# One DMA transpose in place of eight TensorE transposes, for one chunk of a linear-attention and mixer kernel

## The chip, the cores and the metric

The kernel runs on one core of one Trainium2 chip. The metric is device time in microseconds (us) for one launch, as the median of several executions. Lower is better.

## What is computed

The inputs `r`, `k` and `v` have 4 batches, 8 heads, 768 time steps and a head width of 48. First comes a linear attention with a decaying state, then a mixer over tokens and channels. Cut to what matters:

```python
for t in range(S):                      # per batch and head
    cur = (u * k[t]) outer v[t]
    y[t] = r[t] @ (state + cur)
    state = w * state + k[t] outer v[t]
x = y, heads side by side               # 4 x 768 x 384
h = relu(x^T @ w_tok1) @ w_tok2         # mixes the 768 steps
u = x + h^T
out = u + relu(u @ w_ch1) @ w_ch2       # mixes the 384 channels, 1536 hidden
```

## The kernel before

**Tiles.** The 768 steps of a batch are cut into 6 chunks of 128 steps, so there are 24 units (batch, chunk), counted from 0. "Batch 2" below is the third batch, and (2, 0) is its first chunk. A unit computes its chunk of `y` in the following way. `k` and `r` are scaled by powers of the decay (`kr`, half 0 for `k`, half 1 for `r`), both halves are turned so that the head width lies on the partitions (`rk`), and the turned halves are multiplied to scores (`at_ps`) for the 128 x 128 pairs of steps. VectorE masks the scores (`AT`), and TensorE multiplies them by `v` in bf16 (`vb`) and adds the part of the carried state `S` (`y_ps`). The sums of `k` outer `v` go into a bank of PSUM of their own (`kv_ps`), of which there is one; every third chunk of batch 2 closes a group, VectorE makes `S` from the bank, and the next group's first `kv_ps` sums are written into the same bank. A step's own term (`u`) goes another way: GpSimd makes `ku` and `rku`, VectorE sums `rku` per head to `adg`, GpSimd multiplies by `vb` to `yd`, and VectorE adds `yd` to `y_ps` and writes `x_b`.

**The two ways to turn.** The table `STYLES` says for each unit how `k` and `r` are turned. In `unit` (line 815) the style `'pe'` calls `turn_all` (line 903): eight 128 x 128 transposes by TensorE into a PSUM bank (`tr_ps`), and a copy of 128 x 1024 by VectorE or ScalarE into `rk` (`evac`, line 909). The style `'dma'` calls `turn_rk` (line 896): one DMA transpose from SyncE's queue, from `kr` in SBUF to `rk` in SBUF. The style also names who sums the own term; `'dve'` is the same in both.

```python
def turn_rk():
    L["rk"] = sb("rk", [128, 2, HP, T], bf16)
    sp.dma_start_transpose(L["rk"].rearrange("p j a s -> p (j a) s"),
                           L["kr"].rearrange("p j h d -> p (j h d)"))
```

In batches 2 and 3 units go in pairs (`GROUPS`): the scores of (2, 0) and (2, 1) are 16 matmuls in one step, then those of (2, 2) and (2, 3), then (2, 4) and (2, 5). Before the change the two units of the first pair are turned by TensorE, all ten behind them by DMA. In these two batches the products on `k` and `r`, and `ku`, `rku` and `yd`, are on GpSimd (`POOL_ONLY`).

**The mixer** (line 1013) of one batch runs among the attention of the next: `h_ps` stands in the profile for three sums (over `x_b` and `wtok`; over `zr` and `wch`, which is the output; and its addition by `ident`), `hx_ps` and `hT_ps` for the second token matmul, `z_ps` for the hidden channels, `zr` for their relu on ScalarE or VectorE, `osb` for an output tile that SyncE's queue stores. There are three `osb` buffers; a fourth output waits for the store of the buffer that it takes.

**The order.** All steps are recorded as tasks and then issued in the order of a table, `ORDER`; `InOrder` (line 287) keeps that order on each engine, so every instruction has line 287 in the profile. Further tables say which buffer each tile takes (`BUFS`; `m` is the seven banks of PSUM) and, where two engines could do a step, which one does (`ENGINES`). SyncE's queue issues all loads (`kt`, `rt`, `vt`; `win` for two chunks of `r` at once), all DMA transposes and all but one of the stores, one behind the other in this order. A load of `kt`, `rt` or `vt` is 192 KB in rows of 192 bytes; a DMA transpose of one unit is 256 KB.

Of the kernel before, what the change touches and what calls it, by code (L numbers as in the profile page):

```python
# [11 lines left out]
f32 = mybir.dt.float32  # L12
# [6 lines left out]
Ln = ACTF.Ln  # L19

ORDER = [
# [41 lines left out]
]  # L63
BUFS = {
    'AT0': [
# [41 lines left out]
],  # L107
    'osb': [
    0, 1, 2, 2, 1, 0, 2, 1, 2, 0, 1, 2, 0, 2, 0, 1, 0, 1, 2, 1, 0, 2, 1, 0, 2,
# [32 lines left out]
    0, 1, 2, 1, 0, 2,  # L142
],
    'yd': [
    0, 1, 2, 0, 1, 2, 0, 1, 2, 1, 2, 0, 1, 2, 0, 1, 2, 0,
],
    'ydb': [
    0, 1, 0, 1, 0, 1,
# [15 lines left out]
]  # L164
W_DEP = [(0, 2, 2), (0, 5, 0), (0, 5, 0), (0, 3, 2), (1, 2, 0), (1, 1, 2), (1, 3, 0)]
HOLD = {(0, 4, 1): (0, 2, 1),
# [28 lines left out]
 [(0, 1), (2, 3), (4, 5)]]  # L195
STYLES = [
  ('f32', 'pe'), ('f32', 'pe'), ('f32', 'pe'), ('f32', 'pe'), ('f32', 'pe'), ('f32', 'pe'), ('f32', 'pe'),
  ('f32', 'pe'), ('f32', 'pe'), ('f32', 'pe'), ('f32', 'pe'), ('f32', 'pe'), ('pe', 'dve'), ('pe', 'dve'),
  ('dma', 'dve'), ('dma', 'dve'), ('dma', 'dve'), ('dma', 'dve'), ('dma', 'dve'), ('dma', 'dve'),
  ('dma', 'dve'), ('dma', 'dve'), ('dma', 'dve'), ('dma', 'dve'),  # L200
]
# [1038 lines left out]
```

## Time and profile before

| what | value |
|---|---|
| median of 3 runs | 163.56 us (163.2 to 163.7) |
| the profiled execution, its own time | 162.75 us |
| its span, from the first to the last instruction | 161.0 us |
| TensorE busy | 153.0 us (95%), granted clock 0.997 |
| VectorE, GpSimd, ScalarE busy | 113.5, 89.3, 67.7 us |
| bytes moved by DMA | 26.35 MB, mean 164 GB/s |

A row of the timeline gives the start in us from the span's start, the duration, the engine, the operation, the tile written and the tiles read, and in brackets how long the engine had been idle before and what ended that. [...] PE is TensorE (PEld its weight loads), DVE VectorE, ACT ScalarE, POOL GpSimd. Buffer numbers are left out of the names.

### The profile page before, as it was taken

To read this page: it belongs to the slowest core of one execution; us is meant where nothing else is said; L and a number is where in the kernel's file an instruction comes from. 1 tells how busy PE (TensorE), PEld (TensorE's weight loads), DVE (VectorE), ACT (ScalarE), POOL (GpSimd) and SP (SyncE) were. 2 spreads that over 40 slices of the span, in tenths; PEclk is the share of its full clock that TensorE was granted. 3 is DMA by queue.
4 is the path that set the end of the run, shared out by engine and by line. 5 is a ranking of instruction groups with operands and counts; after the bars stand their busy time and mean duration, and the time that the engine had idled before them with its cause. 6 is when DMAs were issued, how large, how long until landed. Compare 5 with 4: busy or idle time off the path is not lost.

```text
span 161.0 us, 3815 instructions
## 1 busy us (share of the span) xinstructions
PE 153.0 (95%) x1475; PEld 102.1 (63%) x1475; DVE 113.5 (70%) x244; ACT 67.7 (42%) x150; POOL 89.3 (55%) x113
## 2 busy tenths in 40 slices
PE   6888789999999999999999999999999999999992
PEld 1354567776666777676776755766667666666661
DVE  6699695767574898789889876788988263852142
ACT  3977985567924243435144241047820202252000
POOL 7049892004788897999999998969422000000000
PEclk9999999999999999999999999999999999999998
DMA  4998899999999999999999997999620157200052
GB/s 124 202 213 165 149 206 211 210 209 196 224 210 211 173 232 178 252 236 171 186 193 224 196 184 150 240 201 197 137 77 4 49 122 219 98 4 0 0 195 98
DMA packets 90948, 26.35 MB, mean 164 GB/s; under 512 B 85682, under 2 KB 90036, under 8 KB 90932
## 3 DMA queue, kind: packets, MB, share of 16 engines
q1 hardware_dynamic: 88576, 22.88, 70.3%
q0 software_dynamic: 2160, 3.15, 11.7%
q8 instruction: 11, 0.18, 0.5%
q10 hardware_dynamic: 196, 0.11, 0.2%
q14 instruction: 5, 0.04, 0.1%
HBM read 20.46 MB, written 4.72 MB: 156 GB/s over the span
## 4 chain that ended last, share of the span: by engine, by line
PE 71%; DMA 10%; issue 9%; POOL 4%; ACT 2%; DVE 1%; SPq 1%; POOLq 0%
PE h_ps L287 34%; PE z_ps L287 23%; DMA vt<-in_v_dram 5%; DMA kt<-in_k_dram 5%; PE y_ps L287 4%; PE hT_ps L287 3%; PE at_ps L287 3%; PE kv_ps L287 2%; POOL wch L287 1%; POOL kr L287 1%; PE hx_ps L287 1%; PE tr_ps L287 1%; POOL pr L287 1%; PE trk L287 1%; ACT vb L287 1%
## 5 line engine op out<-in xcount | busy, mean ns | idle before, releaser
L287 PE MATMUL h_ps<-wch,zr 128*128 128x384 bf16 (+1 forms) x300 | 53.9, 320 | 0.0
L287 PE MATMUL z_ps<-uT,wch 128*128 128x384 bf16 x288 | 51.8, 326 | 0.0
L287 ACT ACTIVATE zr<-z_ps 128x384 bf16<-128x384 f32 x56 | 26.2, 492 | 41.8 <-PE z_ps L287 39.5
L287 PEld LDWEIGHTS <-wch 128*128 128x128 bf16 x288 | 31.4, 114 | 12.5
L287 PEld LDWEIGHTS <-zr 128*128 128x128 bf16 x300 | 27.4, 98 | 15.4 <-issue 0.2
L287 DVE TENSOR_TENSOR AT<-at_ps,mask 128x512 bf16<-128x512 f32 x48 | 30.6, 684 | 3.5 <-PE at_ps L287 2.9
L287 DVE TENSOR_SCALAR zr<-z_ps 128x384 bf16<-128x384 f32 x40 | 21.3, 553 | 12.5 <-PE z_ps L287 12.5
L287 POOL TENSOR_TENSOR kr<-kt,wnat 128x384 bf16<-128x384 f32 x20 | 19.9, 1005 | 2.8 <-DMA kt<-in_k_dram 2.7
L287 POOL TENSOR_TENSOR yd<-vb,adg 128x384 f32<-128x384 bf16 x17 | 13.9, 829 | 8.6 <-DVE x_b L287 4.2
L287 PEld LDWEIGHTS <-kr 128*128 128x128 bf16 x192 | 12.1, 97 | 6.8 <-DVE kr L287 1.8
L287 DVE TENSOR_TENSOR osb<-u_sb,h_ps 128x384 f32<-128x384 bf16 (+1 forms) x16 | 8.2, 526 | 9.7 <-PE h_ps L287 9.5
L287 ACT CAST vb<-vt 128x384 bf16<-128x384 f32 x22 | 11.0, 512 | 5.9 <-DMA vt<-in_v_dram 5.8
L287 POOL TENSOR_TENSOR rku<-ku,rt 128x384 f32<-128x384 f32 x12 | 12.0, 1000 | 0.2
L287 POOL TENSOR_TENSOR ku<-kt,u_bc 128x384 f32<-128x384 f32 x12 | 12.0, 1001 | 0.0
L287 POOL TENSOR_TENSOR kr<-rt,wp 128x384 bf16<-128x384 f32 x12 | 11.9, 1001 | 0.0
L287 DVE TENSOR_TENSOR x_b<-y_ps,yd 128x384 bf16<-128x384 f32 x18 | 9.5, 553 | 3.1 <-PE y_ps L287 1.4
L287 DVE TENSOR_TENSOR u_sb<-x_b,hT_ps 128x384 bf16<-128x384 bf16 x15 | 7.7, 551 | 4.5 <-PE hT_ps L287 4.4
L287 POOL DMA_DIRECT2D wch<-in_moe_w_ch_dram x5 | 3.4, 674 | 13.1 <-DMA kt<-in_k_dram 13.1
L287 PEld LDWEIGHTS <-wtok 128*128 128x128 bf16 x78 | 7.4, 98 | 4.5
L287 PE MATMUL h_ps<-x_b,wtok 128*128 128x384 bf16 x48 | 8.8, 326 | 0.0
L287 PE MATMUL y_ps<-vb,AT 128*128 128x48 bf16 x192 | 8.7, 183 | 0.0
L287 PEld LDWEIGHTS <-AT 128*128 128x128 bf16 x192 | 7.1, 96 | 0.3 <-DVE AT L287 0.2
(96 smaller groups left out, 180.4 us busy)
## 6 DMA issues: line engine op xcount, KB each, us to landing
kt<-in_k_dram SPq DMA_DIRECT2D x24, 192.0 KB, 4.2
vt<-in_v_dram SPq DMA_DIRECT2D x24, 192.0 KB, 4.0
out_dram<-osb SPq DMA_DIRECT2D x23, 192.0 KB, 2.2
win<-in_r_dram SPq DMA_DIRECT2D x6, 384.0 KB, 5.5
rt<-in_r_dram SPq DMA_DIRECT2D x12, 192.0 KB, 4.4
wch<-in_moe_w_ch_dram POOLq DMA_DIRECT2D x4, 384.0 KB, 6.1
wtok<-in_moe_w_tok_dram POOLq DMA_DIRECT2D x2, 384.0 KB, 6.8
wch<-in_moe_w_ch_dram POOLq DMA_DIRECT2D x1, 768.0 KB, 9.1
```

The costliest lines, as they stand in the source:

```text
L287: return lambda *args, **kw: tc.keep_in_program_order(f(*args, **kw))
```

## The change

`STYLES` gives unit 12, which is (2, 0), the style `('dma', 'dve')` in place of `('pe', 'dve')`. The eight transposes and the copy of that unit go, and one DMA transpose comes; there is one task less, so the numbers behind it in `ORDER` fall by one. `ORDER` also moves some steps of the same stretch, and `BUFS` (banks `m` and `yd`) and `ENGINES` follow. Unit (2, 1) is still turned by TensorE.

```diff
 ORDER = [
...
-    306, 411, 414, 407, 412, 394, 307, 416, 532, 429, 536, 89, 330, 415, 92, 422, 533, 395, 417, 419, 431, 313, 88,
+    306, 411, 414, 407, 412, 394, 307, 416, 532, 429, 536, 330, 415, 89, 395, 417, 419, 533, 92, 422, 431, 313, 396,
...
 STYLES = [
-  ('f32', 'pe'), ('f32', 'pe'), ('f32', 'pe'), ('f32', 'pe'), ('f32', 'pe'), ('pe', 'dve'), ('pe', 'dve'),
+  ('f32', 'pe'), ('f32', 'pe'), ('f32', 'pe'), ('f32', 'pe'), ('f32', 'pe'), ('dma', 'dve'), ('pe', 'dve'),
...
```

On SyncE's queue the place is behind the loads of `kt` for (2, 2) and (2, 3), about 60 us into the program. `kr_72` is the buffer with the products of (2, 0), `rk` the turned tile, and `out_dram<-osb` are stores of batch 0.

```order
@@ -27,8 +27,10 @@
 L287 DMA out_dram<-osb 128x384
 L287 DMA kt<-in_k_dram 128x8x48 x2
+L287 DMA_TRANSPOSE rk<-kr_72 128x8x128
 L287 DMA vt<-in_v_dram 128x8x48
+L287 DMA out_dram<-osb 128x384
 L287 DMA rt<-in_r_dram 128x8x48
+L287 DMA out_dram<-osb 128x384
 L287 DMA kt<-in_k_dram 128x8x48
-L287 DMA out_dram<-osb 128x384 x2
 L287 DMA rt<-in_r_dram 128x8x48 x2
 L287 DMA vt<-in_v_dram 128x8x48
```

The new transpose stands ahead of one load of `vt`, and so of all loads, transposes and stores behind that; the two stores, which stood together behind a `kt`, stand apart and earlier, the first ahead of an `rt` and the second ahead of the `kt`.

On VectorE the place is the stretch in which the mixer of batch 1 begins and the first scores of batch 2 are masked. `AT_` with a number is one masked tile of the scores, `u_sb` the mixer's sum, `zr` a relu.

```order
 L287 COPY rk<-tr_ps 128x1024
 L287 CAST uT<-hx_ps 128x3x128
-L287 TENSOR_TENSOR AT_1445<-at_ps,mask 128x512
-L287 TENSOR_TENSOR AT_1455<-at_ps,mask 128x512
 L287 TENSOR_TENSOR u_sb<-x_b_99,hT_ps 128x384
-L287 TENSOR_TENSOR AT_1474<-at_ps,mask 128x512
-L287 TENSOR_SCALAR zr<-z_ps 128x384 x3
+L287 TENSOR_SCALAR zr<-z_ps 128x384
+L287 TENSOR_TENSOR AT_1452<-at_ps,mask 128x512
+L287 TENSOR_TENSOR AT_1461<-at_ps,mask 128x512
+L287 TENSOR_TENSOR AT_1467<-at_ps,mask 128x512
+L287 TENSOR_SCALAR zr<-z_ps 128x384 x2
```

The masks of the first scores stand behind a `u_sb` and the first `zr` and no longer ahead of them, as on TensorE the 16 matmuls of these scores now stand behind four `hT_ps` and two groups of `z_ps`. The copy that is left is that of (2, 1); the one of (2, 0), a few rows further up, is gone. On ScalarE one `zr` moves ahead of a cast of `vb`. GpSimd's order is the same.

More of the change, by code (lines that the diff above doesn't have):

```diff
@@ L144 @@
     'yd': [
-    0, 1, 2, 0, 1, 2, 0, 1, 2, 1, 2, 0, 1, 2, 0, 1, 2, 0,
+    0, 1, 2, 0, 2, 1, 0, 1, 2, 1, 2, 0, 1, 2, 0, 1, 2, 0,
 ],
```

76 rows, old and new, of tables (BUFS, ENGINES, ORDER) are left out of this document.

## Prediction

> **What bounds the kernel now.** I read the page first, for the busiest engine and for the chain that ended last.
>
> ```profile
> span 161.0 us, 3815 instructions
> PE 153.0 (95%) x1475; PEld 102.1 (63%) x1475; DVE 113.5 (70%) x244; ACT 67.7 (42%) x150; POOL 89.3 (55%) x113
> ...
> PE 71%; DMA 10%; issue 9%; POOL 4%; ACT 2%; DVE 1%; SPq 1%; POOLq 0%
> ```
>
> TensorE is busy for 95% of the span and holds 71% of the chain. A share of the whole span does not say what bounds the stretch that the change touches, so the second view is the busy time in windows of 4 us around it. The columns are us, busy us (and count) of PE, PEld, DVE, ACT and POOL, granted clock, DMA share and GB/s.
>
> ```profile
> 64.00:68.00 4.00, 4.00 (x39) 2.86 (x38) 2.83 (x6) 1.75 (x5) 4.00 (x5) 1.00 0.99 242
> 68.00:72.00 4.00, 4.00 (x39) 2.63 (x37) 3.77 (x7) 2.03 (x5) 3.92 (x5) 1.00 1.15 243
> 72.00:76.00 4.00, 4.00 (x32) 2.74 (x31) 3.71 (x8) 1.75 (x5) 4.00 (x5) 1.00 0.93 166
> 76.00:80.00 4.00, 4.00 (x52) 2.84 (x50) 3.02 (x7) 1.27 (x4) 4.00 (x5) 1.00 0.95 180
> ```
>
> Three resources are full at once: TensorE 4.00 of 4 us, GpSimd 3.92 to 4.00, and the DMA engines at a share of 0.93 to 1.15. The end follows TensorE, since after 40 us its matmuls stand in the waits only once:
>
> ```profile
> PE trk L287 <- DVE kr L287: 0.2, 1, 0.2
> ```
>
> So a TensorE instruction that goes is worth its whole time, as long as nothing else comes late. And a DMA or a GpSimd step that slips is free only up to the slack that its reader has. The third view, the timeline of single engines, gives these slacks.
>
> **What goes.** The eight transposes of unit (2, 0) on TensorE, and their copy on VectorE:
>
> ```profile
> 63.21 0.61 PE L287 MATMUL tr_ps<-ident,kr 128*128 128x128 bf16 x8
> 63.66 2.11 PE L287 MATMUL h_ps<-x_b,wtok 128*128 128x384 bf16 x12
> 64.37 0.68 DVE L287 COPY rk<-tr_ps 128x1024 bf16<-128x1024 bf16 x1
> ```
>
> Matmuls overlap at their ends, so the price is start to start: 63.66 - 63.21 = 0.45 us of TensorE. The 12 matmuls behind it read `x_b`, which VectorE finishes by 64.4 us (the copy follows it) in the order that they want it, so starting 0.45 us sooner is possible. The 0.68 us of VectorE lie off the path there. Gain: 0.45 us at most; there is no other TensorE work removed.
>
> **What comes.** One DMA transpose on SyncE's queue, behind the two `kt` at 58.09:
>
> ```profile
> 58.09 1.32 SPq L287 DMA_DIRECT2D kt<-in_k_dram  x2
> 59.46 1.09 SPq L287 DMA_DIRECT2D vt<-in_v_dram  x1
> 60.60 1.72 SPq L287 DMA_DIRECT2D rt<-in_r_dram  x1
> 62.42 0.94 SPq L287 DMA_DIRECT2D kt<-in_k_dram  x1
> 63.41 1.19 SPq L287 DMA_DIRECT2D out_dram<-osb  x2
> 64.64 1.22 SPq L287 DMA_DIRECT2D rt<-in_r_dram  x2
> ...
> 71.36 4.01 SPq L287 DMA_TRANSPOSE rk<-kr  x2
> ...
> 80.22 2.67 SPq L287 DMA_TRANSPOSE rk<-kr  x2
> ```
>
> Its source and its readers:
>
> ```profile
> 57.33 1.00 POOL L287 TENSOR_TENSOR kr<-rt,wp 128x384 bf16<-128x384 f32 x1
> 68.44 0.62 PE L287 MATMUL at_ps<-rk 64*128 64x128 bf16 x16
> ...
> L287 SPq DMA_TRANSPOSE rk<-kr x10: 1232/1284/2666, 71.4 to 112.9; - x10
> DMA to landing us min/median/max: 3.1/3.4/4.7
> ```
>
> GpSimd has the second half of `kr` ready at 58.33, and the issue comes at 59.46. An `rk` lands 3.1 to 4.7 us after its issue, here by about 64, and the scores that read it start at 68.44 before, and behind more work after. So the transpose itself waits for nothing and nobody waits for it. What it costs is the queue. SyncE issues one DMA behind the other with hardly a gap (59.46 + 1.09 = 60.55, next at 60.60), and the engines behind are full, so everything behind 59.46 slips by the time that one transpose takes in the queue. No row isolates that, so I bound it:
>
> ```profile
> q1 hardware_dynamic: 88576, 22.88, 70.3%
> ```
>
> From below, its 256 KB (0.262 MB) at the best window's 243 GB/s are 1.08 us. The queue's mean gives 70.3% of 161.0 us over 88576 packets, 1.28 ns each; if a transpose is as many packets as a load (8 x 128 = 1024), that is 1.3 us. The shortest and the median issue are 1.23 and 1.28 us (the row of `rk<-kr` above, in ns). Of those in the full stretch, the pair at 80.22 took 2.67 us, 1.33 each, and the pair at 71.36 took 4.01 us, 2.0 each, the longest alone 2.67. I take 1.4 us, near most of these rows, and keep 1.08 to 2.0 for the range.
>
> [...]
>
> **Who feels the slip.** First ScalarE: it casts the `vt` issued at 59.46 and does the relu `h1r` behind it.
>
> ```profile
> vt<-in_v_dram SPq DMA_DIRECT2D x1, 192.0 KB, 4.9
> ...
> 64.08 0.93 ACT L287 CAST vb<-vt 128x384 bf16<-128x384 f32 x2
> 65.81 0.49 ACT L287 ACTIVATE h1r<-h_ps 128x384 bf16<-128x384 f32 x1 [0.80 <-PE h_ps L287]
> 67.20 0.49 PE L287 MATMUL hx_ps<-wtok,h1r 128*128 128x384 bf16 x2
> 68.11 0.49 ACT L287 COPY osb<-h_ps 128x384 f32<-128x384 f32 x1
> ```
>
> The `vt` landed at 59.46 + 4.9 = 64.4 and would land at 65.8; cast (0.5) and relu (0.5) are done at 66.8. TensorE wants the relu for the second of the two `hx_ps` matmuls, at 67.20 + 0.16 - 0.45 = 66.9. That is hidden, with nothing to spare; a longer transpose stalls TensorE here. The `osb` at 68.11 needs the second of the stores of 63.41; that store moves up past a `kt` (0.94) and down past the transpose (1.4), some 0.5 us later, so that `osb` may slip to 68.5 and the `uT` cast behind it by as much. The first `z_ps` behind that cast now stands ahead of the scores, at 68.44 - 0.45 and four `hT_ps` of 0.16, so about 68.65; its third matmul at about 69.0 needs the cast, so up to 0.3 us may stall here. These stalls take from the lead of 0.45 and are not added to the next one, which is the larger.
>
> Second GpSimd, through the first of the two `rt` at 64.64, the `r` of (2, 2). The change leaves that load behind the same DMAs as before, and the transpose.
>
> ```profile
> DMA to landing us min/median/max: 3.1/4.4/5.8
> rt<-in_r_dram SPq DMA_DIRECT2D x1, 192.0 KB, 3.8
> ...
> 67.69 1.00 POOL L287 TENSOR_TENSOR ku<-kt,u_bc 128x384 f32<-128x384 f32 x1
> 68.65 1.96 POOL L287 TENSOR_TENSOR kr<-rt,wp 128x384 bf16<-128x384 f32 x2
> ...
> 77.22 1.00 POOL L287 TENSOR_TENSOR rku<-ku,rt 128x384 f32<-128x384 f32 x1
> ...
> 78.25 0.55 DVE L287 TENSOR_REDUCE adg<-rku 128x8 f32<-128x384 f32 x1
> 78.72 0.55 DVE L287 TENSOR_TENSOR S<-kv_ps,wGm 128x384 bf16<-128x384 f32 x1
> ...
> 78.59 0.62 PE L287 MATMUL at_ps<-rk 64*128 64x128 bf16 x16
> ...
> 79.80 0.33 PE L287 MATMUL kv_ps<-vb,kr 128*128 128x96 bf16 x4
> ```
>
> GpSimd uses that `rt` at 68.65 without having waited. Its own landing is not shown: at the earliest 64.64 + 3.1 = 67.74, at the latest 68.65; the next `rt` landed 3.8 us after its issue at 65.22. I take 3.5 us, 68.14, which is 0.5 us of slack (bounds 0 and 0.9). With 1.4 us of slip GpSimd starts that product 1.4 - 0.5 = 0.9 us late. It has no idle time until past 80 (the windows above), so the `rku` of 77.22 ends at 78.22 + 0.9 = 79.1. VectorE's `adg` at 78.25 reads exactly that `rku` (it started 0.03 us behind it), and queued behind `adg` is `S`, which empties the one bank of `kv_ps`: `S` then ends at 79.27 + 0.9 = 80.17. TensorE's `kv_ps` of the next group, at 79.80 before, had 79.80 - 79.27 = 0.53 us of slack. It starts 0.9 - 0.53 = **0.37 us later than before**, though the transposes are gone: the lead of 0.45 us is used up and 0.37 us on top.
>
> Third the scores of (2, 2) and (2, 3) at 78.59, which need the second transpose of the pair at 71.36:
>
> ```profile
> 74.13 1.24 SPq L287 DMA_TRANSPOSE rk<-kr  x1
> ...
> rk<-kr SPq DMA_TRANSPOSE x1, 3.1
> ```
>
> It landed at 74.13 + 3.1 = 77.2 and would land at 78.6, against 78.59 - 0.45 = 78.14. That alone would leave TensorE where it was before; it comes ahead of the `kv_ps`, so the later one counts, not the sum.
>
> Behind 80 us TensorE has the same work as before and, running 0.37 us later, gives every reader that much more slack; the queue gets its time back where SyncE waits for the mixer's `u_sb`. So the sum is 162.75 + 0.37 = 163.1 us for a profiled execution. That execution was 0.8 us below the median of the runs shown, 163.56; on the median I forecast 163.56 + 0.37 = **163.9 us**.
>
> **The rivals.**
>
> *The queue takes it in: faster, 163.1 us.* If the transpose costs no more than 0.5 + 0.53 = 1.03 us of queue, GpSimd's lateness is inside the slacks, the scores' transpose lands at 78.2 and the gain of 0.45 us stays: 163.56 - 0.45. For it: the DMA share falls to 0.93 to 0.99 in three windows, so the queue may have holes that a transpose fills. Against it: the shortest issue of all ten is already 1.23 us, and the byte bound 1.08. [...] Chance 0.23.
>
> *The transpose costs what the pair at 71.36 cost: slower, 164.5 us.* With 2.0 us of slip (or 1.5 us and an `rt` that had landed just in time, with no slack), GpSimd is 1.5 us late and the `kv_ps` 1.5 - 0.53 = 0.97 us: 163.56 + 0.97. It decides from a lateness of GpSimd of 0.53 + 0.49 = 1.02 us on, which is only 0.1 us more than I take. For it: the first transpose of a run of two, ahead of which plain loads stand, was the long one, and the new one stands behind plain loads too; the window of 72 to 76 us has the fewest bytes, 166 GB/s. Against it: the median of the ten issues is 1.28 us. Chance 0.34.
>
> [...]
>
> That the change does not do what it says I leave out: the order shows the transposes gone and the DMA in place.
>
> **How the numbers follow.** The forecast of 163.9 us has a chance of 0.43, the faster rival 0.23, the slower one 0.34. The three runs before spread over 0.5 us, so a measurement can tell about 0.3% (0.49 us) from no change. The forecast, +0.37 us, lies within. The faster rival, -0.45 us, lies at the edge: half of it, 0.12, counts as faster, the rest, 0.11, as the same. So faster 0.12, same 0.43 + 0.11 = 0.54, slower 0.34. The range reaches from the whole gain, 163.1, to a lateness of 1.6 us, 163.56 + 1.6 - 0.53 = 164.6; the likeliest case's own range, with 1.1 to 1.5 us of slip, is 163.6 to 164.1.
>
> **What would show it.** Right: the eight `tr_ps` and one copy gone and `h_ps<-x_b` 0.45 us sooner; the two `rt` issued 1.2 to 1.6 us later; GpSimd idle for about 0.9 us ahead of a `kr<-rt`, with DMA as the releaser; VectorE waiting for GpSimd ahead of an `adg`, and the `kv_ps` behind the scores of (2, 2) no earlier than before. Wrong: GpSimd without that gap, or the scores of (2, 2) starting near 78.1, which is the faster rival; a gap of 1.5 us, which is the slower one; or a TensorE stall ahead of 70 us that alone exceeds 0.45 us, which would mean that ScalarE and not GpSimd carries the slip.

## The result and the profile after

The changed kernel is slower: 165.04 us median (164.5 to 165.6) against 163.63 for the kernel before beside it (163.2 to 163.75), a ratio of 1.0105 with a 95% interval of 1.0064 to 1.0145. The forecast was 163.9 with a range up to 164.6. The profiled execution took 164.5 us with a span of 162.8, against 162.75 and 161.0, so it shows 1.8 us of loss. The interval lies clear of 1; the loss is about 1% of the time.

First TensorE's waits after 40 us. The kernel before had only the `trk` row; three kinds have come.

```profile
PE at_ps L287 <- DMA rk<-kr: 0.8, 2, 0.5
PE hx_ps L287 <- ACT h1r L287: 0.6, 1, 0.6
PE trk L287 <- DVE kr L287: 0.2, 1, 0.2
PE kv_ps L287 <- DVE S L287: 0.2, 1, 0.2
```

Next SyncE's queue (SPq) in the timeline (start, duration of the issue). The row of 59.59 is the new transpose.

```profile
58.10 1.40 SPq L287 DMA_DIRECT2D kt<-in_k_dram  x2
59.59 3.31 SPq L287 DMA_TRANSPOSE rk<-kr  x1
62.96 0.57 SPq L287 DMA_DIRECT2D vt<-in_v_dram  x1
63.59 0.57 SPq L287 DMA_DIRECT2D out_dram<-osb  x1
64.20 0.43 SPq L287 DMA_DIRECT2D rt<-in_r_dram  x1
64.67 0.71 SPq L287 DMA_DIRECT2D out_dram<-osb  x1
65.43 0.43 SPq L287 DMA_DIRECT2D kt<-in_k_dram  x1
65.91 2.58 SPq L287 DMA_DIRECT2D rt<-in_r_dram  x2
...
73.79 3.75 SPq L287 DMA_TRANSPOSE rk<-kr  x2
...
82.49 2.70 SPq L287 DMA_TRANSPOSE rk<-kr  x2
```

Its issue took 3.31 us where the prediction took 1.4. The `vt` behind it starts 3.5 us later than before (62.96 against 59.46); the `rt` of (2, 2), five places further, only 1.3 us later (65.91 against 64.64); the pair of transposes for (2, 2) and (2, 3) is 2.4 us later again (73.79 against 71.36). So the slip is not one number for the whole queue. The landing was long as well; the DMA view of that stretch has

```profile
q8 instruction: 1, 0.02, 0.8%
...
rk<-kr SPq DMA_TRANSPOSE x1, 5.2
```

that is 5.2 us from issue to landing, with an instruction fetch (queue q8) in the same stretch. The windows of one us show that the DMA engines moved little just then; the last two columns are the DMA share and GB/s.

```profile
61.00:62.00 1.00, 1.00 (x21) 0.74 (x18) 0.91 (x3) 0.48 (x2) 0.94 (x2) 1.00 1.67 222
62.00:63.00 1.00, 1.00 (x20) 0.74 (x17) 0.97 (x2) 0.00 (x0) 0.45 (x1) 1.00 2.03 65
63.00:64.00 1.00, 1.00 (x11) 0.68 (x10) 1.00 (x3) 0.62 (x2) 0.69 (x1) 1.00 0.47 106
64.00:65.00 1.00, 1.00 (x8) 0.61 (x7) 0.38 (x1) 0.51 (x1) 1.00 (x2) 1.00 0.60 114
```

Who then came late, in the timelines of ScalarE, GpSimd and VectorE:

```profile
66.17 0.51 ACT L287 CAST vb<-vt 128x384 bf16<-128x384 f32 x1 [1.64 <-DMA vt<-in_v_dram]
66.70 0.49 ACT L287 ACTIVATE h1r<-h_ps 128x384 bf16<-128x384 f32 x1
...
70.28 1.97 POOL L287 TENSOR_TENSOR kr<-rt,wp 128x384 bf16<-128x384 f32 x2 [1.19 <-DMA rt<-in_r_dram]
...
79.90 0.55 DVE L287 TENSOR_REDUCE adg<-rku 128x8 f32<-128x384 f32 x1 [1.07 <-POOL rku L287]
80.37 0.55 DVE L287 TENSOR_TENSOR S<-kv_ps,wGm 128x384 bf16<-128x384 f32 x1
```

ScalarE waits for the `vt`, and the relu `h1r` stands behind that cast. GpSimd starts `kr<-rt` at 70.28 instead of 68.65, and VectorE's `adg` waits for GpSimd. On TensorE:

```profile
67.41 0.49 PE L287 MATMUL hx_ps<-wtok,h1r 128*128 128x384 bf16 x2
...
79.52 0.62 PE L287 MATMUL at_ps<-rk 64*128 64x128 bf16 x16 [0.28 <-DMA rk<-kr]
...
81.06 0.33 PE L287 MATMUL kv_ps<-vb,kr 128*128 128x96 bf16 x4 [0.16 <-DVE S L287]
...
88.88 0.62 PE L287 MATMUL at_ps<-rk 64*128 64x128 bf16 x16 [0.53 <-DMA rk<-kr]
```

To compare kernels that run some tenths apart from the start, I take the start of a TensorE group, less the start of the last `kv_ps` ahead of the change (63.04 before, 62.97 after), and subtract the same for the kernel before. For the scores of (2, 2) after: (79.52 - 62.97) - (78.59 - 63.04) = +1.00 us. Negative is ahead of the kernel before. The other columns are the runs below.

| TensorE group, its start before | after | no transpose | extra one | old order | five later | two later | loads behind | new queue |
|---|---|---|---|---|---|---|---|---|
| `h_ps` over `x_b`, 63.66 | -0.45 | -0.44 | 0.00 | -0.45 | -0.45 | -0.45 | -0.45 | -0.45 |
| first `hx_ps` that needs `h1r`, 67.20 | +0.28 | -0.44 | 0.00 | -0.25 | -0.44 | -0.44 | -0.44 | +0.09 |
| `kv_ps`, 72.09 | +0.67 | -0.13 | +1.25 | +1.24 | -0.14 | -0.09 | -0.03 | +1.53 |
| scores of (2, 2), 78.59 | +1.00 | -0.10 | +1.25 | +1.23 | +0.46 | +0.58 | -0.04 | +1.53 |
| next group's `kv_ps`, 79.80 | +1.33 | -0.10 | +1.25 | +1.24 | +0.47 | +0.98 | -0.03 | +1.53 |
| scores of (2, 4), 87.02 | +1.93 | +0.01 | +1.42 | +1.24 | +1.12 | +1.19 | +0.25 | +1.52 |
| scores of (3, 0), 100.75 | +1.87 | -0.04 | +1.37 | +1.23 | +1.06 | +1.13 | +0.20 | +1.52 |

The lead of 0.45 us is there at 63 us. It is lost at `h1r` (0.73), and more is lost up to 72 us (0.39), at the scores of (2, 2) (0.33), at `kv_ps` (0.33) and at the scores of (2, 4) (0.60). From there nothing changes.

### The profile page after: what moved, and what is told of

Read it like the earlier page. It is cut to its first block, busy times and chain, and to the rows that moved or that the text cites. A ratio compares the mean times of both kernels' runs of the same rounds, so it can differ in the third digit from the quotient of the medians.

```text
span 162.8 us, 3798 instructions
## 1 busy us (share of the span) xinstructions
PE 153.7 (94%) x1467; PEld 101.8 (63%) x1467; DVE 112.8 (69%) x243; ACT 67.9 (42%) x150; POOL 89.4 (55%) x113
## 4 chain that ended last, share of the span: by engine, by line
PE 59%; DMA 16%; issue 9%; POOL 8%; ACT 3%; SPq 2%; DVE 1%; POOLq 0%
PE h_ps L287 31%; PE z_ps L287 17%; DMA kt<-in_k_dram 8%; DMA vt<-in_v_dram 5%; POOL kr L287 4%; PE y_ps L287 3%; DMA rk<-kr 3%; PE hT_ps L287 3%; PE at_ps L287 2%; POOL yd L287 2%; SPq L287 2%; POOL wch L287 1%; PE kv_ps L287 1%; PE hx_ps L287 1%; POOL pr L287 1%
## 5 line engine op out<-in xcount | busy, mean ns | idle before, releaser
L287 DVE TENSOR_REDUCE adg<-rku 128x8 f32<-128x384 f32 x12 | 6.4, 545 | 1.5 <-POOL rku L287 1.5
```

What stands on the lines that cost most here:

```text
L287: return lambda *args, **kw: tc.keep_in_program_order(f(*args, **kw))
```

## The experiments

Theory Q: the DMA transpose delays what stands behind it in SyncE's queue, and the loss comes through the readers of those DMAs. Rival O: the new order of scores, stores and loads costs the time. A further question was why the issue was so long: theory F, because an instruction fetch met it; rival L, because plain loads were queued ahead of it. Ratios are to the kernel before on the same chip, with 95% intervals.

**No transpose.** The changed kernel with that one step left out: the scores of (2, 0) read a constant tile instead of `rk`.

```diff
 def turn_rk():
+    if n == 12:
+        plan.buf("rk")
+        L["rk"] = warm.rearrange("p (o a t) -> p o a t", o=1, a=HP)
+        return
     L["rk"] = sb("rk", [128, 2, HP, T], bf16)
```

> The changed kernel without its DMA transpose: the scores of (2, 0) read the constant zero tile `warm` instead of `rk`, so the scores of that chunk are left out; the moved order stays, and so do all loads and stores. Theory Q (the transpose delays all that stands behind it in SyncE's queue): without it the 0.45 us of TensorE remain as a gain, 163.63 - 0.45 = 163.2 us, `vt` issued near 59.5 as before, no wait of TensorE for `h1r`, `kv_ps` at 79.8 - 0.45 = 79.4 us. Rival O (the order in which scores, stores and loads now stand costs the time, the transpose itself does not): stays near 165.0 us, and `kv_ps` near 81.1.

Measured: 0.9996 (0.9962 to 1.003). The loss is gone, so the transpose carries it and rival O falls as the main cause. But the gain that Q left over does not show either: in the table 0.44 us are there at 67 us and 0.13 at 72 us. TensorE and VectorE in that stretch:

```profile
70.12 1.94 PE L287 MATMUL z_ps<-uT,wch 128*128 128x384 bf16 x9
71.90 0.33 PE L287 MATMUL kv_ps<-vb,kr 128*128 128x96 bf16 x4
```

```profile
70.03 1.89 DVE L287 TENSOR_TENSOR AT<-at_ps,mask 128x512 bf16<-128x512 f32 x3 [0.29 <-PE at_ps L287]
```

Nine `z_ps` matmuls take 71.90 - 70.12 = 1.78 us from start to start; before, twelve took 72.09 - 70.14 = 1.95, 0.1625 each, so nine should take 1.46. The 0.32 us between are lost at a `z_ps` that takes a bank of PSUM out of which VectorE must first mask the scores (`AT`): it waits for a semaphore of VectorE and starts at 71.38, right behind the end of the second mask at 71.32. The scores now come later, and three masks stand in a row up to 71.92 us. That is the price of the new order, 0.3 us, with no transpose in the queue.

**An extra transpose.** All of the kernel before, and a transpose of the same `kr` that nobody reads, ahead of the `vt` load (88 in the order).

```diff
+ extra.append((lambda: sp.dma_start_transpose(spare, L["kr"]...), [t_kp, t_rp]))
+ plan.order.insert(plan.order.index(88), 910)
```

> The kernel before, with all its TensorE transposes, its order and its scores, plus one DMA transpose of the same `kr` into a tile that nobody reads, at the place in SyncE's queue where the change puts its own (behind the two `kt` of 58 us, ahead of `vt`). Theory Q: the queue slips as in the changed kernel, TensorE has no 0.45 us to give, so 163.63 + 1.4 (after less before) + 0.45 = about 165.5 us, 164.8 to 166; an issue of about 3.3 us if theory F holds as well (the issue is long since an instruction fetch falls into it: the fetch comes at 60.4 us here too), about 1.4 us if it does not. Rival O: 163.6 us, no change.

Measured: 1.0071 (1.0037 to 1.0105), about 1.2 us: all else is the kernel before, so the one added DMA costs that. The issue took 3.20 us and the landing 5.4, as in the changed kernel.

```profile
59.63 3.20 SPq L287 DMA_TRANSPOSE wnpair<-kr  x1
```

The path is another one, though: in the table 1.25 us are lost between 67 and 72 us, nothing more at `kv_ps`, and 0.17 at the scores of (2, 4). The next run but one shows why.

**An extra load.** As above, with a plain load of 192 KB in place of the transpose.

```diff
+ extra.append((lambda: sp.dma_start(spare, k[b, :, ts(c, T), :]...), [t_kp, t_rp]))
```

> As the run with the extra transpose, but with a plain load of 192 KB of k in its place, which nobody reads. Theory F (a fetch and a transpose together stop the DMA engines, a fetch and a load do not): no second with under 150 GB/s between 60 and 65 us, an issue of 0.6 to 1.0 us, and a time of 163.6 to 164.1 us, since 0.8 us of slip is within the slacks of 0.5 us at `rt` and 0.5 us at `S`. If it is the bytes in the queue and not the transpose: 3/4 of its loss, about 165 us.

Measured: 1.0036 (1.0004 to 1.0067), 0.6 us, half of what the transpose costs. The issue took 1.88 us, more than expected, and the expectation that no window of 1 us (the "second" there) falls under 150 GB/s failed:

```profile
59.77 1.88 SPq L287 DMA_DIRECT2D spare<-in_k_dram  x1
```

```profile
62.00:63.00 1.00, 1.00 (x20) 0.83 (x18) 0.97 (x2) 0.00 (x0) 0.72 (x2) 1.00 0.59 112
```

So the DMA engines sag here with plain loads as well, in one window and not in three. The kernel before has 142 GB/s in this window, and the control run at the end, which has no new transpose, 33 GB/s. F holds in weaker form: the dip is longer with a transpose, not absent without.

**The transpose in the old order.** The DMA transpose at its place in the queue, with scores, stores and loads as in the kernel before.

```diff
  SyncE:  kt, kt,
+         transpose (2, 0),
          vt, rt, kt, out, out, rt, rt, ...
  TensorE:
-         tr_ps (2, 0)
          ... scores (2, 0), (2, 1), hT_ps, z_ps ...
```

> The transpose by DMA at the same place in SyncE's queue, but all else in the order of the kernel before: the scores of (2, 0) and (2, 1) ahead of the four `hT_ps` at about 68 us, the stores where they stood, the loads behind the transpose in the old order. Theory Q: 164.6 to 165.5 us, as the changed kernel or a little worse since the scores come 2 us sooner behind a landing at 64.8. Rival O: 163.2 us, the gain without the loss.

Measured: 1.0089 (1.0055 to 1.0122), within errors the changed kernel's 1.0105. So the transpose loses as much without the new order, by another path. VectorE's timeline, then TensorE's:

```profile
67.53 0.56 DVE L288 COPY osb<-h_ps 128x384 f32<-128x384 f32 x1 [2.28 <-DMA out_dram<-osb]
...
68.46 0.68 DVE L288 COPY rk<-tr_ps 128x1024 bf16<-128x1024 bf16 x1
```

```profile
68.14 0.38 PE L288 MATMUL at_ps<-rk 64*128 64x128 bf16 x7 [0.42 <-DVE osb L288]
69.20 0.40 PE L288 MATMUL at_ps<-rk 64*128 64x128 bf16 x8 [0.68 <-DVE rk L288]
```

VectorE waits 2.28 us for a store that slipped behind the transpose, since `osb` takes that store's buffer. Behind it waits the copy of (2, 1), and TensorE waits 0.42 + 0.68 = 1.10 us for both. The new order avoids this path (the scores come later, one store sooner) and pays elsewhere.

**Five places later.** The changed kernel with the transpose behind the `rt` of (2, 2) (93 in the order), which stands five places behind the `vt`; six DMAs in all now go ahead of it.

```diff
+ plan.order.remove(537)
+ plan.order.insert(plan.order.index(93) + 1, 537)
```

> The changed kernel with the transpose moved five places back in SyncE's queue: behind `vt`, both stores, the first two `rt` and a `kt`, at about 65.6 us; its readers, the scores at 69.6 to 70.4, leave it 4 us to land. Theory Q: no stall at `h1r` (0.7 us less), GpSimd's `kr<-rt` back near 68.6, but the loads and the pair of transposes behind slip; the scores of (2, 2) want that pair at 78.4 and it lands there without slack, so 0.4 to 0.9 us are lost there: with the 0.45 us of gain and the 0.3 us that the order costs, 163.6 + 0.2 to 0.7 us, some 1 us faster than the changed kernel. Theory F (a transpose that an instruction fetch meets takes 2 us more in the queue): the transpose at 65.6 takes 1.3 us and not 3.3. If it takes 3 us here too, plain loads ahead of it make it long, not the fetch.

Measured: 1.005 (1.002 to 1.008). As Q says, there is no stall at `h1r`, and GpSimd's `kr<-rt` starts at 68.41, with no wait. What stays is at the two pairs of transposes that stand behind the new one:

```profile
PE at_ps L287 <- DMA rk<-kr: 1.1, 2, 0.6
```

0.60 us at the scores of (2, 2) and 0.65 at those of (2, 4). The issue here took

```profile
64.80 2.08 SPq L287 DMA_TRANSPOSE rk<-kr  x1
```

and no fetch fell between 64.5 and 69 us. That lies between F's 1.3 and L's 3, so by this issue neither alone gives the length.

**Fetches shifted.** To move the fetches away, each warming matmul of 512 columns was cut into four.

```diff
-  pe.matmul(bank[0][:, 512 - cols:512], warm[:, 0:128], warm[:, 0:cols], ...)
+  for q in range(4):
+      pe.matmul(bank[0][:, ts(q, 128)], warm[:, 0:128], warm[:, 0:128], ...)
```

> The changed kernel with each of its twelve warming matmuls of 512 columns, all ahead of 16 us, cut into four of 128: the same columns, 36 more pairs of TensorE instructions, so that each instruction fetch comes 36 pairs sooner, about 3 us: 57.7, 70.1 and 82.9 us in place of 60.8, 73.8 and 86.3. Theory F: the transpose issued at 59.6 meets no fetch, takes 1.3 us in the queue and lands after 3.1 to 3.5 us; the loss shrinks from 1.9 us to 0.4 to 0.9 us, 164.0 to 164.5 on the scale where the kernel before has 163.6. Rival L (the plain loads queued ahead of it make it long): it takes 2.5 to 3.3 us as in the changed kernel, and the time stays at 165.0.

Measured: 1.0179 (1.0127 to 1.023). The control has the same lines in the kernel before:

```diff
-  pe.matmul(bank[0][:, 512 - cols:512], warm[:, 0:128], warm[:, 0:cols], ...)
+  for q in range(4):
+      pe.matmul(bank[0][:, ts(q, 128)], warm[:, 0:128], warm[:, 0:128], ...)
```

> The control of the run before: the same cut of the warming matmuls in the kernel before. Its transposes had slack, so neither theory sees more than 0.3 us of change: 163.3 to 163.9 on the scale where the kernel before has 163.6.

Measured: 1.0111 (1.0072 to 1.0151), with 2.1 us of wait for one `trk` before 50 us. The cut itself costs about 1.8 us, all of it ahead of the change, so as an experiment on time this pair failed, and so did the third of the kind, the transpose five places later with the cut:

```diff
+ plan.order.insert(plan.order.index(93) + 1, 537)
...
+  for q in range(4):
```

> The transpose five places later and the fetches 3 us sooner, both. Theory F: no transposes of the stretch from 65 to 79 us meet a fetch (57.7, 70.1, 82.9 us), the pair for (2, 2) and (2, 3) lands before its readers, and what stays is the 0.45 us of gain less the 0.3 us that the order costs: 163.3 to 163.6 us, no slower than the kernel before. Rival L: the long issue stays, and 0.4 us or more are lost at the scores of (2, 2), 164 us or more.

Measured: 1.0135 (1.0088 to 1.0181). Two things can still be read. With no fetch between its issue and its landing, the transpose of the first of these took 2.02 us and landed after 3.9.

```profile
60.65 2.02 SPq L287 DMA_TRANSPOSE rk<-kr  x1
```

Yet its `kv_ps` waited 1.2 us for `S`. The `rt` of (2, 2) was issued 0.66 us sooner than in the changed kernel ((65.73 - 63.45) - (65.91 - 62.97)), but now a fetch, at 68.82, fell into its landing, which took 5.6 us, and GpSimd waited for it:

```profile
71.36 1.96 POOL L287 TENSOR_TENSOR kr<-rt,wp 128x384 bf16<-128x384 f32 x2 [1.79 <-DMA rt<-in_r_dram]
```

A shorter issue alone does not save the time. Second, in the count of the table the last of the three stays 0.14 us ahead of the kernel before at the scores of (2, 2) and 0.15 at those of (3, 0), and the control stays at 0.00. That is the gain less the price of the order, as its expectation had it. It does not single out the fetch: TensorE had been held up at the start, so the queue stood 1.2 us further ahead of it than with the transpose five places later alone ((64.54 - 64.60) - (63.94 - 62.77) for that `rt`).

**Two places later.** Behind `vt` and a store (312 in the order), with the `rt` of (2, 2) still behind it.

```diff
+ plan.order.remove(537)
+ plan.order.insert(plan.order.index(312) + 1, 537)
```

> The changed kernel with the transpose two places back, behind `vt` and a store, at about 61.8 us; the `rt` of (2, 2) stays behind it. The instruction fetch at about 60.4 us is over by then. Theory F: 2.0 us in the queue and a landing 3.8 to 4.0 us after the issue, where the changed kernel had 3.3 and 5.2; if plain loads ahead alone decide, 2.6 to 3.3 us. Theory Q on the path: no wait of TensorE for `h1r`, but `kr<-rt` on GpSimd still 1.2 to 1.6 us late and `kv_ps` with it, 0.6 to 1.0 us behind where it stood before; in all 164.3 to 164.9 us on the scale where the kernel before has 163.6, between the run with five places (164.4) and the changed kernel (165.3).

Measured: 1.0082 (1.0051 to 1.0113), 1.3 us. The rows of the queue:

```profile
58.96 2.13 SPq L287 DMA_DIRECT2D vt<-in_v_dram  x1
61.14 0.79 SPq L287 DMA_DIRECT2D out_dram<-osb  x1
62.03 1.37 SPq L287 DMA_TRANSPOSE rk<-kr  x1
...
65.23 2.05 SPq L287 DMA_DIRECT2D rt<-in_r_dram  x2
```

The transpose now takes 1.37 us and lands after 3.2; the fetch, and the long issue, fell on the `vt` (2.13 us, against 0.57 in the changed kernel). No wait for `h1r`, but

```profile
69.38 1.95 POOL L287 TENSOR_TENSOR kr<-rt,wp 128x384 bf16<-128x384 f32 x2 [1.22 <-DMA rt<-in_r_dram]
```

GpSimd still waits for that `rt`, and `kv_ps` is 0.98 us behind. This separates the two paths: what stands directly behind the transpose loses through `h1r`, the `rt` further behind through GpSimd and `S`.

**Loads behind the pairs.** Five places later, and two `kt` with slack moved behind the pairs of transposes.

```diff
  SyncE:
-         vt, kt, transposes (2, 2), (2, 3), kt, uT, ..., transposes (2, 4), (2, 5)
+         vt, transposes (2, 2), (2, 3), kt, uT, ..., transposes (2, 4), (2, 5), kt
```

> The transpose five places back, and two `kt` with 4.5 and 15 us of slack moved behind the two pairs of transposes that came late there (0.6 and 0.65 us of TensorE at the scores of (2, 2) and of (2, 5)). Theory Q (the slip reaches TensorE through these pairs, as they stand behind it in the queue): both stalls shrink to under 0.2 us each, and what is left is the gain of 0.45 less the order's 0.3 to 0.4: 163.5 to 163.9 us on the scale where the kernel before has 163.6. If the pairs were late for another reason (the DMA engines full, a fetch), the stalls stay and the time is 164.4 as without this move.

Measured: 1.0031 (0.9997 to 1.0064): level with the kernel before within the errors, and 0.7% better than the changed one. Its interval overlaps that of the run five places later (1.002 to 1.008), so the time alone does not show a gain over that. The waits after 40 us:

```profile
PE trk L288 <- DVE kr L288: 0.2, 1, 0.2
PE at_ps L288 <- DMA rk<-kr: 0.2, 1, 0.2
```

The stall at (2, 2) is gone, that at (2, 4) fell from 0.65 to 0.28 us. So the slip did reach TensorE through these pairs. Its last matmul ends at 157.70 us (157.81 before), which counted as in the table is (157.70 - 62.26) - (157.81 - 63.04) = 0.67 us behind, so 0.47 us more are lost after 100 us; what causes that was not followed.

**The old order with a queue made for it.** Here the old order of the scores keeps the masks apart, and the queue is laid out so that what slips has slack; two `kt` go behind the pairs, as in the run before.

```diff
  SyncE:
-         kt, kt, transpose (2, 0), vt, rt, kt, out, out, rt, rt, ...
+         kt, kt, vt, out, out, rt of (2, 2), transpose (2, 0), rt, kt, rt, ...
```

> The transpose by DMA with the scores where they stood in the kernel before, and a queue laid out for it: `vt`, both stores and the `rt` of (2, 2) first, then the transpose at about 63.8 us, then the loads with slack, and the two `kt` behind the pairs. By theory Q no reader of the queue is late: the transpose lands at 67.7 us, where the scores want it at 68.0, and the whole 0.45 us stay as a gain, 163.2 us on the scale where the kernel before has 163.6, so the version that beats both. If the DMA engines and not the queue's order are what is full, something else comes late, and it is 163.6 us or more.

Measured: 1.0064 (1.0037 to 1.0092); Q's expectation failed, and the outcome is the one written down there for engines that are full whatever the order. The control has the kernel before, its TensorE transposes among it, and the same queue without the transpose:

```diff
  SyncE:
-         kt, kt, vt, rt, kt, out, out, rt of (2, 2), rt, ...
+         kt, kt, vt, out, out, rt of (2, 2), rt, kt, rt, ...
```

> The control of the run before: the kernel before, with its TensorE transposes, and that same queue without the transpose. TensorE waited for nothing there, so the new queue alone brings nothing: 163.4 to 163.8 us on the scale where the kernel before has 163.6.

Measured: 1.0007 (0.9971 to 1.0043), as expected. So by the times the transpose costs 0.6% in this queue too. In the trace it comes by yet another reader:

```profile
PE z_ps L288 <- ACT zr L288: 1.0, 1, 1.0
```

```profile
71.53 0.51 ACT L288 CAST vb<-vt 128x384 bf16<-128x384 f32 x1 [3.07 <-DMA vt<-in_v_dram]
71.95 0.48 ACT L288 ACTIVATE zr<-z_ps 128x384 bf16<-128x384 f32 x1
```

In the old order ScalarE's cast of a `vt` stands ahead of a relu `zr`, and that `vt` slipped: it was issued 1.16 us later than in the control ((67.31 - 62.39) - (66.49 - 62.73)). The changed order has the two the other way round. Whether full engines or the place in the queue made it late, these two runs do not separate. The traces here are a coarser measure than the times: that of the control is of an execution 0.8 us above its median, and in the count of the table it is itself 0.96 us behind at the scores of (3, 0), with short waits of its own, where the run with the transpose is 1.52. None of the versions run here beats the kernel before.

## Why the prediction was wrong

The direction of the mechanism held: a gain of 0.45 us on TensorE and a loss through the queue. Two steps failed: the one price of 1.4 us for the transpose, passed on alike to every reader, where the issue took 3.31 us; and the end of the walk at `kv_ps`, where the queue stayed late and cost TensorE again. Step by step:

- **"Gain: 0.45 us at most"**: right, -0.45 in the table at 63 us.
- **"I take 1.4 us ... and keep 1.08 to 2.0"**: too little, and not one number. The `vt` directly behind was issued 3.5 us later, as it had the whole long issue ahead of it. Where the `rt` of (2, 2) is issued the slip looks about right, (65.91 - 62.97) - (64.64 - 63.04) = 1.34 us, as the issues ahead of it had become short (0.57 us for the `vt`, 1.09 before). But that `rt`'s own issue then took 1.44 us against 0.48 before, and the pairs of transposes behind it were issued (73.79 - 62.97) - (71.36 - 63.04) = 2.50 and (82.49 - 62.97) - (80.22 - 63.04) = 2.34 us late. In the old order the slip is 1.32 us at the `rt` and 1.50 at the first pair ((72.16 - 62.34) - (71.36 - 63.04)), near the forecast; so a part of the rest belongs to the new order, in which that `rt` takes 1.40 us to issue even without the transpose.
- **"That is hidden, with nothing to spare"** (`vt`, `h1r`): the sentence named the place and its condition, a longer transpose, and that came: 0.73 us of TensorE.
- **"I take 3.5 us" for the landing of that `rt`**: it landed 70.21 - 65.91 = 4.3 us after its issue. With that GpSimd was (70.28 - 62.97) - (68.65 - 63.04) = 1.70 us late, counted as in the table, and not 0.9. In the old order it was 0.96 us late (68.91 - 62.34 against 68.65 - 63.04), nearly the forecast. The landing itself is not slower in the new order: from the end of the `rt`'s issue it took 70.21 - (65.91 + 1.44) = 2.9 us there and, in the old order, where it landed at 68.84, 68.84 - (65.26 + 0.45) = 3.1; it is the issue of 1.44 us against 0.45 that makes the difference. Why that issue is longer in the new order stays open.
- **The chain GpSimd, `adg`, `S`, `kv_ps` with 0.53 us of slack**: right. 1.70 - 0.53 = 1.17 against +1.33 measured; two places later, 69.38 - 62.42 against 68.65 - 63.04 gives 1.35 late, 0.82 against +0.98.
- **"up to 0.3 us may stall here"** (`osb`, `uT`): 0.3 us were lost there even without the transpose, but by VectorE's masks holding a bank of PSUM, a cost of the new order that the prediction did not see.
- **"Behind 80 us ... gives every reader that much more slack; the queue gets its time back"**: wrong. The queue got nothing back at the `u_sb`: the transpose of `uT` that reads it was issued (78.26 - 62.97) - (76.10 - 63.04) = 2.23 us late and the pair behind it 2.34, as above, and 0.60 us more were lost at the scores of (2, 4).
- **The sign "a TensorE stall ahead of 70 us that alone exceeds 0.45 us"** came, at `h1r`. It did not mean, as said there, that ScalarE and not GpSimd carries the slip: both do. Two places later that stall is gone, and `kv_ps` is still 0.98 us behind.
- **"at the best window's 243 GB/s are 1.08 us"**, the bound from below: 243 is the best of the windows of 4 us shown there; of those of 1 us in the same trace, the one from 65 to 66 us has 355 GB/s, at which the 0.262 MB take 0.74 us. So the bound did not speak against the faster rival (1.03 us); the shortest issue of the ten, 1.23 us, did. Neither the sum nor the outcome changes by it.

The trace of the kernel before held a warning. The issue of 2.67 us that the prediction names as the longest had an instruction fetch in it, at 71.61 us, and another fetch came at 60.37 us, where the new transpose was to stand. The first of the two, in the DMA view of 71.4 to 72 us before:

```profile
q8 instruction: 1, 0.02, 10.1%
...
rk<-kr SPq DMA_TRANSPOSE x1
```

The range ended at 164.6, as it stopped at `kv_ps`. The rival with the dearer transpose (2.0 us of slip) had the right place and nearly the size up to there (+0.97 us forecast, +1.33 measured); what neither had is the second loss behind it.

## What to carry to other kernels

The DMA added to the full queue here was not one delay but one for each reader (3.5 us where the `vt` is issued, 1.3 at the `rt` of (2, 2), 2.5 and 2.3 at the pairs of transposes): walk the queue behind it and hold each landing, not each issue, against its first reader, down to the last transfer ahead of a real gap. Where order and operation change together, leave the operation out once: the order's own price here (0.3 us) took most of the gain of 0.45. Loads with slack that stand ahead of tight transfers are a place to win some of it back: here two stalls of 0.60 and 0.65 us in the trace fell to none and 0.28, though the times (1.0050 and 1.0031) overlap. And look in the trace of the kernel before for what already comes by at the place where the new DMA is to stand.

## What the runs showed of the hardware

An instruction fetch (in the trace before, 11 on queue q8 with 0.18 MB, 16 KB each, and 5 on q14 with 0.04 MB, 8 KB each) went with a long issue of what SyncE was issuing then in several places. In the changed kernel it fell on the transpose, 3.31 us; two places later it fell on `vt`, 2.13 us; in the control run on `vt` again, 2.63 us, and the window of 1 us behind it moves only 33 GB/s:

```profile
62.00:63.00 1.00, 1.00 (x17) 0.70 (x15) 0.97 (x3) 0.53 (x2) 0.00 (x0) 1.00 0.19 33
```

The two fetches of 60.75 and 73.78 us stand 131 matmuls and 130 weight loads apart in the windows, and the next at 86.30 a further 123 and 122:

```profile
60.75:73.78 13.03, 12.38 (x131) 8.37 (x130) 9.96 (x18) 5.28 (x13) 10.85 (x12) 1.00 1.11 205
73.78:86.30 12.52, 12.08 (x123) 8.35 (x122) 9.80 (x21) 4.95 (x13) 12.52 (x15) 1.00 1.07 199
```

so 261 and 245 recorded instructions of TensorE lie between one and the next. The cut of the warming matmuls points to these instructions as what brings a fetch: 36 more pairs of them were expected to bring each fetch about 3 us sooner, and the one at the change came (60.75 - 62.97) - (58.49 - 63.45) = 2.74 us sooner.

A transpose during whose issue a fetch began landed after 5.2, 5.4 and 4.9 us (changed kernel, extra transpose, old order); at nearly the same place without one, after 3.2 to 4.0 us (two later, five later, loads behind, fetches shifted). The fourteen traces together have 149 of these transposes of `kr`, and they agree. A fetch began during the issue, or less than 0.1 us ahead of it, in 36 of them, which took 1.25 to 3.41 us; the 113 others took 1.23 to 2.18. All 17 issues above 2.2 us are among the 36. The traces give 92 landings: the 48 with no fetch between issue and landing took 3.0 to 4.1 us, the 44 with one 3.1 to 5.5, and all 33 above 4.1 us have one. So every issue above 2.2 us and every landing above 4.1 us among these met a fetch, but not every fetch came with one. Whether and how a fetch lengthens them is not shown, as the run meant to move the fetches alone moved the start as well.

TensorE is busy for 1.00 of each of the four windows from 61 to 65 us above, right behind the fetch of 60.75 us; what is long there is SyncE's issue, 3.31 us.
